# A two-part kernel (chunked scan, then a gated feed-forward layer): decays of first tokens scanned before they are spread, one load of C on ScalarE, three landing times in the planner

## The chip, the cores and the metric

The kernel runs on one core of a Trainium2 chip. The metric is the device time of one execution in microseconds (us), the median of three runs. The core has five engines with their own instruction queues, each strictly in order: PE (TensorE, matmuls; its weight loads are shown apart as PEld), DVE (VectorE), ACT (ScalarE), POOL (GpSimd) and SP (SyncE, which here issues loads and stores). Transfers run on 16 DMA engines.

## The reference

Inputs are x (4, 8, 768, 32), a (4, 8, 768), B and C (4, 8, 768, 16) and three weight matrices (256x1536, 256x1536, 1536x256). A gated linear recurrence runs over each of 32 heads in chunks, and its output, as 3072 tokens of 256 values, goes through a gated feed-forward layer.

```python
log_a = np.log(np.clip(a, 1e-06, 1.0))
for c in range(nc):                               # chunks of a sequence
    cum = np.cumsum(la, axis=-1)
    L = np.exp(cum[:, :, :, None] - cum[:, :, None, :]) * causal
    M = np.einsum('bhin,bhjn->bhij', Cc, Bc) * L
    y_inter = np.einsum('bhin,bhnd->bhid', Cc, state) * np.exp(cum)[..., None]
    y[:, :, sl] = np.einsum('bhij,bhjd->bhid', M, xc) + y_inter
    Bx = (Bc outer xc) * exp(cum[-1] - cum)
    state = exp(sum(la)) * state + sum(Bx)
g = x @ w_gate
out = (g * sigmoid(g) * (x @ w_val)) @ w_out
```

## The kernel before, in words

**Blocks.** The 768 tokens of a sequence are cut into six blocks (k = 0 to 5) of 128 tokens, each of two pieces (q = 0, 1) of 64. A block holds all 4 batches and 8 heads, so it has 512 tokens for the feed-forward layer.

**The scan of a block.** `L` holds the decays between the tokens of a piece, one column row per target token: a row of clipped `a` values is put on all 128 partitions and a `tensor_tensor_scan` with the identity `dj` turns it into products from each source token on (`scan_j`, four scans of 128x520). `E` holds the decays from a piece's first token: the same row for every partition of a head, scanned with `dn` (`scan_n`, one scan of 128x520). B is weighed with the last column of `L` (`weigh_b`), C with `E` (`weigh_c`). `heads_apart` writes C twice, with one or the other head of a pair blanked (`Cz`). PE then makes the scores S, DVE mixes them with `L` (`mix`, four a block), PE makes values and sums of the pieces (the first group of y matmuls), ACT or DVE takes the states T apart, DVE steps them, PE adds what is carried in (the second group of y matmuls).

**How the decays arrive.** For block 0 eight rows of 520 values (`rows`) are loaded twice, clipped, and put on the partitions by a matmul with a 0/1 table `pick` (`spread`, 2 x 4 halves of 260 columns); a ninth such matmul spreads the row that `E` of block 0 is scanned from. For the later blocks everything is loaded once (`all`, 128 partitions x 2 x 195 values), clipped on POOL, written to DRAM (`clipped`), and from there broadcast into `L` (`load_aj`, two transfers) and `E` (`load_an`).

**The feed-forward layer.** f32 weights come as 64-bit words and are taken apart on ACT and DVE into a rounded high part and a low part (per weight piece wg0 to wg11, wo0 to wo5: `w_magnitude`, `w_rest` on ACT, `w_range` on POOL or DVE, `w_shift`, `w_sign`, `w_round` on DVE; the last is the CUSTOM_DVE or ISA row). gate_val makes the gate and the value of weight piece f: in block 0, for the first nine pieces, as two f32 products with the whole x (`xf`) of 4 matmuls, which the profile shows as 8 passes; later as 12 passes of high and low parts (`xh`, `xl`). `silu` is on ACT and `product` on DVE, both into `sg`; they free the two PSUM banks of the piece. There are four such banks, so gate_val of piece f needs silu and product of piece f - 2. `project` makes the output (`po`).

**What sets the order.** Nothing is in program order: every step is an entry `add(engine, cost, run, rank, needs, takes, ...)` of a planner (`Plan`, lines 45 to 180), which keeps a clock for each engine and always issues the step that can start first, by rank among those that can start together. A cost, a rank, a need or a landing time (`lag`) that changes moves steps on all engines. `plan.follow([...])` chains named steps in a fixed order (the lists at lines 949 to 958 and `ORDER`). SP issues the weight loads wg0 to wg11 and the loads of block 1 in the order of `ORDER`. `IDLE` are matmuls on constants ("rest") without a use for the result; lines 963 to 985 hold these tables.

Of the kernel before, what the change touches and what calls it, by code (L numbers as in the profile page):

```python
# [9 lines left out]
F32 = mybir.dt.float32  # L10
# [34 lines left out]
class Plan:  # L45
# [156 lines left out]
def scan_moe_kernel(ctx: ExitStack, tc, aj, an, bc, xb, wgv, wo, cst, own, out):  # L202
# [21 lines left out]
    pick = const.tile([64, BATCH + 1, P], F32, name="pick")  # L224
# [52 lines left out]
    def write_all(e, rows):  # L277
        t = bl[0]["all"][rows].rearrange("p i a t -> p i (a t)")
        e.dma_start(clipped[:, rows].rearrange("i p c -> p i c"), t)
# [12 lines left out]
    def clip(t):  # L292
        ve.tensor_scalar(t, t, 1e-6, 1.0, ALU.max, ALU.min)
# [5 lines left out]
    def scan(t, d):  # L299

        ve.tensor_tensor_scan(t, t, d, 0.0, ALU.mult, ALU.add)

    def clip_rows(i):
        t = bl[0]["rows"]
        t = t[32 * i : 32 * i + H, 0] if i < 2 else t[:H, 1]
        t = t.rearrange("p (g t) -> p g t", t=W)
        clip(t[:, :, 1:] if i < 2 else t[:, 1::K, 1:])
# [3 lines left out]
    def first(b, i):  # L311
        return b < BATCH and not i

    def spread(b, i):

        where, tag = (ps_mm, "mm") if first(b, i) else (ps_at, "at")
        t = bl[0]["spread", b, i] = where.tile([P, HALF], F32, tag=tag, name=f"a{b}_{i}")
        half = slice(HALF * i, HALF * i + HALF)
        if b < BATCH:
            rows = slice(32 * (b % 2), 32 * (b % 2) + H)  # L320
            te.matmul(t, pick[rows, b], bl[0]["rows"][rows, 0, half], start=True, stop=True)
        else:
            r = bl[0]["rows"][:H, 1].rearrange("p (b q t) -> p b q t", b=BATCH, q=K)[:, :, 1]
            te.matmul(t, pick[:H, b], r, start=True, stop=True)

    def scan_spread(b, i):
        if b < BATCH:
            to, d = bl[0]["L"][:, H * b : H * b + H].rearrange("p g t -> p (g t)"), dj
        else:
            to, d = bl[0]["E"].rearrange("p b q t -> p (b q t)"), dn  # L330
        half = slice(HALF * i, HALF * i + HALF)
        d = d.rearrange("p g t -> p (g t)")[:, half]
        ve.tensor_tensor_scan(to[:, half], bl[0]["spread", b, i], d, 0.0, ALU.mult, ALU.add)

# [399 lines left out]
    def do(f, *a):  # L734
        return lambda *e: f(*a, *e)
# [72 lines left out]
    add("SP", 0.48, do(write_all, sp, slice(0, FEW)), -9, ["clipped"], gives="few", lag=2.6)  # L808
    add("Act", 0.1, do(write_all, se, slice(FEW, P)), -1.6, ["clipped", ("rest", 0)], gives="written", lag=0.3)


    for k in range(NB):
# [18 lines left out]
        if not k:  # L831
            add("-", 0.0, lambda: None, -9, takes=[("xl", "rows")], gives="rows", lag=0.2)
            for i in range(3):
                add("DVE", 0.35, do(clip_rows, i), (-9, -8.9, -5)[i], ["rows", *([("scan0", 1)] if i == 2 else [])], gives=("clip", i))
            for b in range(BATCH + 1):
                r = z + 0.5 + b if b < BATCH else -1.3
                for i in range(2 if b < BATCH else 1):
# [74 lines left out]
    for k in range(NB):  # L912
# [39 lines left out]
        ("spread", BATCH, 0), *(("idle", 1, i) for i in range(len(IDLE[1]))), *(("st", 0, b) for b in range(BATCH)),  # L952
# [5 lines left out]
    plan.follow([("L", 0, b) if i else ("scan0", b) for b, i in halves] + [("bt", 0), ("M", 0, 0), ("M", 0, 1), ("E", 0), ("M", 0, 2), ("ce", 0), ("M", 0, 3), ("shift", 0), ("sign", 0, "gate"), ("round", 0, "gate"), ("sign", 0), ("round", 0), ("range", 1)])  # L958
# [4 lines left out]
CST = 2 + 2 * D  # L963
NA = NB * K * BATCH * H // P
IDLE = [-9.0] * 6, [-4.0] * 2
IDLE_AFTER = [], [("spread", BATCH, 0)]
# [12 lines left out]
    [("raw", 8), ("bc", 1), ("raw", 9), ("aj", 1), ("raw", 10), ("xb", 1), ("raw", 11), ("an", 1)],  # L979
# [61 lines left out]
```

## Time and profile before

| | |
|---|---|
| three runs | 351.43, 351.07, 348.14 us, median 351.07 |
| the profiled execution | 349.64 us, span from first to last instruction 347.6 us |
| PE busy | 339.9 us (98%) |
| DVE, ACT, POOL busy | 229.5, 123.7, 44.7 us (66%, 36%, 13%) |
| granted TensorE clock, mean | 1.000 |
| chain that ended last | PE 84%, DMA 5%, DVE 3%, ACT 3% |

The chain of waits is read from the end backwards: whatever released an instruction stands in front of it. From 53.33 us on it consists of PE alone up to the last copy of the output. Timelines give start, duration and, in brackets, the idle time of the engine before the instruction with what ended it. Neighbouring instructions of one kind are merged into one row with their count. A matmul's end is modelled, so the distance between starts is the better measure of PE.

### The profile page before, as it was taken

To read this page: it belongs to the slowest core of one execution; us is meant where nothing else is said; L and a number is where in the kernel's file an instruction comes from. 1 tells how busy PE (TensorE), PEld (TensorE's weight loads), DVE (VectorE), ACT (ScalarE), POOL (GpSimd) and SP (SyncE) were. 2 spreads that over 40 slices of the span, in tenths; PEclk is the share of its full clock that TensorE was granted. 3 is DMA by queue.
4 is the path that set the end of the run, shared out by engine and by line. 5 is a ranking of instruction groups with operands and counts; after the bars stand their busy time and mean duration, and the time that the engine had idled before them with its cause. 6 is when DMAs were issued, how large, how long until landed. Compare 5 with 4: busy or idle time off the path is not lost.

```text
span 347.6 us, 7425 instructions
## 1 busy us (share of the span) xinstructions
PE 339.9 (98%) x3196; PEld 266.3 (77%) x3196; DVE 229.5 (66%) x417; ACT 123.7 (36%) x227; POOL 44.7 (13%) x36
## 2 busy tenths in 40 slices
PE   7999989999999999999999999999999999999996
PEld 6644447888878888878888888888878888888895
DVE  6997999788999792686573676465676430565320
ACT  3795946654336602222322212232212221222221
POOL 2397735322022000000000000000000000000000
PEclk9999999999999999999999999999999999999999
DMA  7999855992001841000561000381000000100001
GB/s 259 294 364 258 231 114 123 272 258 79 0 2 44 190 136 61 0 2 3 152 156 60 0 2 2 100 208 60 1 3 2 2 2 0 60 2 0 0 2 60
DMA packets 9935, 30.98 MB, mean 89 GB/s; under 512 B 1287, under 2 KB 2055, under 8 KB 9263
## 3 DMA queue, kind: packets, MB, share of 16 engines
q1 hardware_dynamic: 7168, 24.23, 23.3%
q0 software_dynamic: 1440, 2.88, 4.9%
q10 hardware_dynamic: 1295, 3.40, 3.2%
q8 instruction: 25, 0.41, 0.5%
q14 instruction: 7, 0.06, 0.1%
HBM read 24.28 MB, written 3.35 MB: 79 GB/s over the span
## 4 chain that ended last, share of the span: by engine, by line
PE 84%; DMA 5%; DVE 3%; ACT 3%; issue 1%; ACTq 0%; DVEq 0%
PE gv L191 50%; PE po L191 29%; PE y L191 4%; DMA wg9r<-in_wgv 4%; PE S L191 1%; DMA wo1r<-in_wo 1%; DVE L L191 1%; DVE wg1w L191 1%; DVE wg0w L191 1%; DVE wg9w L191 0%; DVE sg L191 0%; ACT sg L191 0%; ACT wg9w L191 0%; DVE wg8w L191 0%; DVE E L191 0%
## 5 line engine op out<-in xcount | busy, mean ns | idle before, releaser
L191 DVE TENSOR_TENSOR sg<-gv,sg 128x512 f32<-128x512 f32 x72 | 49.6, 689 | 75.5 <-PE gv L191 73.2
L191 ACT ACTIVATE sg<-gv 128x512 f32<-128x512 f32 x72 | 42.9, 596 | 104.7 <-PE gv L191 104.7
L191 DVE TENSOR_TENSOR hh<-sg,hh 128x512 fp32r<-128x512 f32 x72 | 49.6, 691 | 14.1 <-ACT hh L191 12.8
L191 ACT CAST hh<-sg 128x512 fp32r<-128x512 f32 x32 | 19.9, 622 | 27.1 <-PE po L191 17.5
L191 DVE TENSOR_TENSOR_SCAN L<-L,dj 128x520 f32<-128x520 f32 x20 | 23.9, 1229 | 1.9 <-DMA L<-clipped 1.9
L191 ACT COPY ob<-po 128x512 f32<-128x512 f32 (+1 forms) x13 | 7.2, 555 | 48.7 <-PE po L191 48.2
L191 DVE CAST hh<-sg 128x512 fp32r<-128x512 f32 x40 | 17.4, 435 | 2.4 <-PE po L191 1.2
L191 DVE TENSOR_TENSOR L<-S,L 128x512 f32<-128x512 f32 x24 | 15.2, 684 | 0.3 <-PE S L191 0.3
L191 PE MATMUL po<-hh,wo3h 128*128 128x512 f32 (+1 forms) x52 | 15.2, 375 | 0.0
L191 PE MATMUL po<-hh,wo1h 128*128 128x512 f32 (+1 forms) x52 | 15.2, 375 | 0.0
L191 PE MATMUL po<-hh,wo0h 128*128 128x512 f32 (+1 forms) x52 | 15.2, 375 | 0.0
L191 PE MATMUL po<-hh,wo4h 128*128 128x512 f32 (+1 forms) x52 | 15.1, 373 | 0.0
L191 PE MATMUL po<-hh,wo5h 128*128 128x512 f32 (+1 forms) x52 | 15.1, 373 | 0.0
L191 PE MATMUL po<-hh,wo2h 128*128 128x512 f32 (+1 forms) x52 | 15.0, 373 | 0.0
L191 PE MATMUL y<-L,xb 64*32 64x64 f32 x768 | 11.2, 231 | 0.9 <-DVE L L191 0.9
L191 PEld LDWEIGHTS y<-L,xb 64*32 64x32 f32 x768 | 9.0, 109 | 3.8 <-issue 3.2
L191 PEld LDWEIGHTS po<-hh,wo0h 128*128 128x128 f32 x52 | 9.5, 188 | 1.9 <-issue 0.2
L191 PEld LDWEIGHTS po<-hh,wo4h 128*128 128x128 f32 x52 | 9.5, 188 | 1.7
L191 PEld LDWEIGHTS po<-hh,wo2h 128*128 128x128 f32 x52 | 9.5, 188 | 1.7
L191 PEld LDWEIGHTS po<-hh,wo5h 128*128 128x128 f32 x52 | 9.5, 188 | 1.7
L191 PEld LDWEIGHTS po<-hh,wo3h 128*128 128x128 f32 x52 | 9.4, 188 | 1.8
L191 PEld LDWEIGHTS po<-hh,wo1h 128*128 128x128 f32 x52 | 9.4, 188 | 1.8
(298 smaller groups left out, 750.5 us busy)
## 6 DMA issues: line engine op xcount, KB each, us to landing
L<-clipped SPq DMA_DIRECT2D x10, 520.0 KB, 14.3
xb<-in_xb SPq DMA_DIRECT2D x6, 768.0 KB, 11.2
bc<-in_bc SPq DMA_DIRECT2D x6, 512.0 KB
out<-ob SPq DMA_DIRECT2D x11, 256.0 KB, 2.0
E<-clipped SPq DMA_DIRECT2D x5, 260.0 KB
wg0r<-in_wgv SPq DMA_DIRECT2D x1, 512.0 KB
wg1r<-in_wgv SPq DMA_DIRECT2D x1, 512.0 KB
wg2r<-in_wgv SPq DMA_DIRECT2D x1, 512.0 KB
```

The costliest lines, as they stand in the source:

```text
L191: ins = getattr(self.engine, name)(*a, **k)
```

## The change

The decays from a piece's first token are now scanned once and before they are spread. For blocks 1 to 5 DVE scans the 195 values of each of the 128 partitions of `all[:, 1]` in one instruction (`scan_all`), and ACT writes the result to `clipped[1]`; `load_an` then brings finished decays, so `scan_n` is gone. It waits for that second write ("written e"). For block 0 a new input `first_e` holds 32 rows (batch and head) of 65 values and a 0/1 table; the rows are clipped and scanned as 32x65 (`first_row`), spread by four matmuls of 65 columns into one bank (`spread_e`), and copied to `E` by ACT (`copy_e`). Of the two wide idle matmuls one is left.

`heads_apart` of block 1 may go to ACT alone. `weigh_b` is one instruction for all four batches of a block. The landing times of wg9, of block 1's `L` and of wg10 are given to the planner as 6.1, 2.4 and 1.9 instead of 1.3, 4.8 and 1.3, and a few chains of order are changed. The feed-forward layer is as it was.

```diff
     def load_rows():
...
-        sp.dma_start(t[:H, 1], an[0])
+        sp.dma_start(t[E_ROWS, :W], first_e[:, BATCH * P :])
+        se.dma_start(pick[E_ROWS], first_e[:, : BATCH * P].rearrange("m (b p) -> m b p", p=P))
...
+    def first_row():
+        t = bl[0]["rows"][E_ROWS, :W]
+        clip(t[:, 1:])
+        scan(t, dn[E_ROWS, 0])
+
+    def scan_all():
+        scan(bl[0]["all"][:, 1].rearrange("p a t -> p (a t)"), dn[:, :NA].rearrange("p a t -> p (a t)"))
...
+    def spread_e():
+        t = bl[0]["e"] = ps_at.tile([P, BATCH * W], F32, tag="at", name="e0")
+        for b in range(BATCH):
+            te.matmul(
+                t[:, W * b : W * b + W], pick[E_ROWS, b], bl[0]["rows"][E_ROWS, :W],
+                start=True, stop=True,
+            )
+
+    def copy_e():
+        se.copy(second(bl[0]["E"]).rearrange("p b t -> p (b t)"), bl[0]["e"])
...
-    def scan_n(k):
-
-        scan(bl[k]["E"].rearrange("p b q t -> p (b q t)"), dn.rearrange("p g t -> p (g t)"))
...
-            add("SP", 0.48, do(w_fetch, i), r - 9.0, takes=[("raw", ("raw", i))], gives=("raw", i), lag=1.3)
+            add("SP", 0.48, do(w_fetch, i), r - 9.0, takes=[("raw", ("raw", i))], gives=("raw", i), lag=SHARED.get(i, 1.3))
...
-    add("Act", 0.1, do(write_all, se, slice(FEW, P)), -1.6, ["clipped", ("rest", 0)], gives="written", lag=0.3)
+    add("Act", 0.1, do(write_all, se, 0, slice(FEW, P)), -1.6, ["clipped", ("rest", 0)], gives="written", lag=0.3)
+    add("DVE", 0.48, scan_all, due(0, 1), ["clipped"], gives="products")
+    add("Act", 0.1, do(write_all, se, 1, slice(0, P)), due(0, 1) - 2, ["products"], gives="written e", lag=0.3)
...
+            add("PE", 0.5, spread_e, -1.3, ["row"], takes=[("at", "e")], uses=["e", "rows"], gives="e", kind="s")
+            add("Act", 0.35, copy_e, -1.7, ["e", ("decays", 0)], uses=["e"], gives=("E", 0))
...
-            add("DVE", 1.17, do(scan_n, k), z + 6, [("an", k)], gives=("E", k), slack=SLOW.get(k, 1.0))
...
+        add("DVE", 0.61, do(weigh_b, k), z + 4.5 if k else -1.2, [*(("L", k, b) for b in range(BATCH)), ("xb", k)], gives=("bt", k), slack=SLOW.get(k, 0.0))
+        add([("Act", 1.2)] if k == 1 else [("Act", 1.35), ("DVE", 0.72)], None, do(heads_apart, k), z, [("bc", k)], takes=[("Cz", CZ)], gives=("Cz", k))
...
+E_ROWS = slice(64, 64 + BATCH * H)
-IDLE = [-9.0] * 6, [-4.0] * 2
+IDLE = [-9.0] * 6, [-4.0]
...
+    [("step", 0, 1), "products", ("sign", 2)],
+    [("mag", 6), "written e", ("rest", 7)],
+    [("raw", 8), ("bc", 1), ("raw", 9), ("aj", 1), ("raw", 10), ("xb", 1), ("raw", 11), ("E", 1)],
...
-    [("round", 6), ("Cz", 1)],
+    [("si", 0, 2), ("Cz", 1)],
...
+SHARED = {9: 6.1, "aj": 2.4, 10: 1.9}
```

Three places show what this moves. First DVE in block 0, from the weighing of B to the first weight piece (xb is B and x, bc is B and C, S the scores, a the spread rows), before:

```order
L191 TENSOR_TENSOR xb_100<-xb_100,L_96 128x4x128
L191 TENSOR_TENSOR L_96<-S_0_182,L_96 128x4x2x64
L191 TENSOR_TENSOR L_96<-S_1_183,L_96 128x4x2x64
L191 SCALAR_TENSOR_TENSOR E_97<-a_0_225,dn 128x260
L191 TENSOR_TENSOR L_96<-S_2_184,L_96 128x4x2x64
L191 TENSOR_TENSOR bc_98<-bc_98,E_97 128x4x64
L191 TENSOR_TENSOR L_96<-S_3_185,L_96 128x4x2x64
L191 TENSOR_SCALAR wg0w<-wg0w 128x512
```

and now:

```order
L191 TENSOR_TENSOR xb_101<-xb_101,L_97 128x4x128
L191 TENSOR_TENSOR L_97<-S_0_182,L_97 128x4x2x64
L191 TENSOR_TENSOR L_97<-S_1_183,L_97 128x4x2x64
L191 TENSOR_TENSOR bc_99<-bc_99,E_98 128x4x64
L191 TENSOR_TENSOR L_97<-S_2_184,L_97 128x4x2x64
L191 TENSOR_TENSOR L_97<-S_3_185,L_97 128x4x2x64
L191 TENSOR_SCALAR wg0w<-wg0w 128x512
```

The scan into E left this queue, and the weighing of C moved ahead of the third mix; it now waits for ACT's copy of E. On PE, the one spread matmul and the two wide idle matmuls between the scores and the sums became four narrow spread matmuls and one idle matmul.

Second, ACT from the silu of piece 2 to that of piece 4 and on (xh is the high part of x, wgNh and wgNl high and low parts of weights), before:

```order
L191 ACTIVATE sg_2_466<-gv_2_0_444 128x512
L191 CAST xh_387<-xf 128x512
L191 ACTIVATE wg9w<-wg9r 128x512
L191 ACTIVATE wg9r<-wg9r 128x512
L191 CAST xh_387<-xf 128x512
L191 CAST wg0h<-wg0w 128x512
L191 ACTIVATE sg_3_488<-gv_3_0_473 128x512
```

and now:

```order
L191 ACTIVATE sg_2_469<-gv_2_0_445 128x512
L191 ACTIVATE Cz_473<-bc_437,cs 128x4x128 x2
L191 ACTIVATE wg8r<-wg8r 128x512
L191 CAST xh_389<-xf 128x512 x2
L191 ACTIVATE sg_3_491<-gv_3_0_477 128x512
L191 CAST wg0h<-wg0w 128x512
L191 ACTIVATE wg0l<-wg0w 128x512
L191 CAST wg1h<-wg1w 128x512
L191 ACTIVATE wg1l<-wg1w 128x512
L191 CAST wg2h<-wg2w 128x512
L191 ACTIVATE sg_4_516<-gv_4_0_499 128x512
L191 ACTIVATE wg9w<-wg9r 128x512
```

The two steps on wg9, which wait for its load, stood ahead of the silu of piece 3 and stand behind that of piece 4 now; block 1's Cz, which waits for the load of bc, came in ahead of the silu of piece 3.

Third, DVE in block 0 from the product of piece 4 on, where block 1's decays are scanned, before:

```order
L191 TENSOR_TENSOR sg_4_516<-gv_4_1_513,sg_4_516 128x512
L191 TENSOR_TENSOR xb_452<-xb_452,L_376 128x128 x2
L191 SCALAR_TENSOR_TENSOR L_376<-L_376,dj 128x520
L191 ISA wg7w<-wg7r,wg7w 128x1024
L191 TENSOR_TENSOR xb_452<-xb_452,L_376 128x128
L191 TENSOR_TENSOR sg_5_541<-gv_5_1_536,sg_5_541 128x512
L191 SCALAR_TENSOR_TENSOR L_376<-L_376,dj 128x520
L191 SCALAR_TENSOR_TENSOR E_377<-E_377,dn 128x520
L191 TENSOR_TENSOR xb_452<-xb_452,L_376 128x128
L191 SCALAR_TENSOR_TENSOR wg8w<-wg8r,wg8w 128x512
L191 TENSOR_TENSOR bc_429<-bc_429,E_377 128x512
L191 ISA wg8w<-wg8r,wg8w 128x1024
```

and now, from the rounding of piece 8 on:

```order
L191 ISA wg8w<-wg8r,wg8w 128x1024
L191 TENSOR_TENSOR sg_4_516<-gv_4_1_512,sg_4_516 128x512
L191 SCALAR_TENSOR_TENSOR L_379<-L_379,dj 128x520 x3
L191 TENSOR_TENSOR sg_5_541<-gv_5_1_537,sg_5_541 128x512
L191 SCALAR_TENSOR_TENSOR L_379<-L_379,dj 128x520
L191 TENSOR_SCALAR wg9w<-wg9w 128x512
L191 TENSOR_TENSOR xb_460<-xb_460,L_379 128x4x128
L191 SCALAR_TENSOR_TENSOR wg9w<-wg9r,wg9w 128x512
L191 TENSOR_TENSOR L_379<-S_0_549,L_379 128x4x2x64
L191 TENSOR_TENSOR sg_6_607<-gv_6_1_603,sg_6_607 128x512
L191 ISA wg9w<-wg9r,wg9w 128x1024
L191 TENSOR_TENSOR bc_437<-bc_437,E_380 128x512
```

Pieces 7 and 8 are rounded ahead of all scans of block 1 now, the scan of E is gone, and the weighing of C stands between the first and the second mix.

## Rows read from the trace of the kernel before

**Rows 1.** The page's part 1: busy us (share of the span), xinstructions.
```profile
PE 339.9 (98%) x3196; PEld 266.3 (77%) x3196; DVE 229.5 (66%) x417; ACT 123.7 (36%) x227; POOL 44.7 (13%) x36
```

**Rows 2.** Waits of PE: waiting line <- releaser: us in total, times, longest.
```profile
PE y L191 <- DVE L L191: 0.9, 1, 0.9
```

**Rows 3.** Timeline of PE alone: start, us, instruction, count [idle before <-releaser].
```profile
19.08 3.60 PE L191 MATMUL gv<-xf,wg1w 128*128 128x512 f32 x8
22.71 3.67 PE L191 MATMUL gv<-xf,wg2w 128*128 128x512 f32 x8
26.22 3.60 PE L191 MATMUL gv<-xf,wg3w 128*128 128x512 f32 x8
29.66 3.60 PE L191 MATMUL gv<-xf,wg4w 128*128 128x512 f32 x8
33.50 3.70 PE L191 MATMUL gv<-xf,wg5w 128*128 128x512 f32 x8 [0.25 <-ACT sg L191]
...
41.80 3.60 PE L191 MATMUL gv<-xf,wg7w 128*128 128x512 f32 x8
45.66 3.67 PE L191 MATMUL gv<-xf,wg8w 128*128 128x512 f32 x8 [0.26 <-DVE wg8w L191]
49.26 0.60 PE L191 MATMUL y<-L,xb 64*32 64x64 f32 x18
...
52.04 0.50 PE L191 MATMUL gv<-xh,wg9h 128*128 128x512 f32 x1
53.33 0.39 PE L191 MATMUL gv<-xh,wg9h 128*128 128x512 f32 x1 [0.78 <-issue]
```

**Rows 4.** The chain of waits: start, us, what; the same y group in block 2, and 24 passes.
```profile
102.74 1.41 PE y L191 x90
104.16 5.68 PE po L191 x24
```

**Rows 5.** Timeline of all engines in the first 12 us.
```profile
4.81 1.88 DVE L191 TENSOR_TENSOR_SCAN L<-a,dj 128x260 f32<-128x260 f32 x3 [1.14 <-PE a L191]
...
6.60 0.26 DVE L191 TENSOR_SCALAR rows<-rows 8x256 f32<-8x256 f32 x1
...
9.50 0.50 PEld L191 LDWEIGHTS a<-rows,pick 8*128 8x128 f32 x2 [0.33 <-DVE L L191]
...
10.67 1.03 PE L191 MATMUL rest<-unit 128*128 128x512 bf16 x2
...
11.63 1.15 PE L191 MATMUL st<-xb 64*32 64x64 f32 x62
11.66 0.69 DVE L191 TENSOR_TENSOR_SCAN E<-a,dn 128x260 f32<-128x260 f32 x1
```

**Rows 6.** Busy time by stretch: PE, PEld, DVE, ACT, POOL, PEclk, DMA share, GB/s.
```profile
19.00:22.60 3.60, 3.60 (x9) 1.33 (x7) 3.60 (x11) 3.18 (x6) 3.60 (x3) 1.00 1.02 410
```

**Rows 7.** Timeline, DVE: rounding of weight piece 2.
```profile
21.89 0.68 DVE L191 CUSTOM_DVE_ANT_0 wg2w<-wg2r,wg2w 128x1024 uint16<-128x1024 uint16 x1
```

**Rows 8.** Timeline of all engines, 30 to 46 us: ACT and DVE.
```profile
30.67 0.69 ACT L191 ACTIVATE wg9w<-wg9r 128x512 f32<-128x512 f32 x1 [3.96 <-DMA wg9r<-in_wgv]
30.70 0.88 DVE L191 TENSOR_SCALAR Cz<-bc,cs 128x512 f32<-128x512 f32 x2
...
35.35 2.37 DVE L191 TENSOR_TENSOR_SCAN L<-L,dj 128x520 f32<-128x520 f32 x2
...
44.83 0.69 DVE L191 CUSTOM_DVE_ANT_0 wg8w<-wg8r,wg8w 128x1024 uint16<-128x1024 uint16 x1
```

**Rows 9.** The page: instruction fetches (packets, MB, share); a load (count, KB each, us to landing).
```profile
q8 instruction: 25, 0.41, 0.5%
...
L<-clipped SPq DMA_DIRECT2D x10, 520.0 KB, 14.3
```

**Rows 10.** Timeline of PE alone: the scores of block 0 and of block 1.
```profile
7.57 2.01 PE L191 MATMUL S<-Cz,bc 32*64 32x128 f32 x64
...
37.13 1.21 PE L191 MATMUL S<-Cz,bc 32*64 32x128 f32 x64
```

More of the change, by code (lines that the diff above doesn't have):

```diff
@@ L223, in scan_moe_kernel @@
     step_of = const.tile([P, W], F32, name="step")
-    pick = const.tile([64, BATCH + 1, P], F32, name="pick")
+    pick = const.tile([P, BATCH, P], F32, name="pick")
     dj = const.tile([P, H, W], F32, name="dj")
@@ L275, in load_all, with write_all @@
             sp.dma_start(t[:, i], rows)
-    def write_all(e, rows):
-        t = bl[0]["all"][rows].rearrange("p i a t -> p i (a t)")
-        e.dma_start(clipped[:, rows].rearrange("i p c -> p i c"), t)
+    def write_all(e, i, rows):
+        e.dma_start(clipped[i, rows], bl[0]["all"][rows, i].rearrange("p a t -> p (a t)"))
     def load_bc(k):
@@ L303, in clip_rows @@
     def clip_rows(i):
[L304 to L307, printed above, removed]
+        clip(bl[0]["rows"][32 * i : 32 * i + H].rearrange("p (g t) -> p g t", t=W)[:, :, 1:])
+    def first_row():
[4 more added lines that the diff above has]
+        scan(bl[0]["all"][:, 1].rearrange("p a t -> p (a t)"), dn[:, :NA].rearrange("p a t -> p (a t)"))
@@ L309, in scan_moe_kernel, with first @@
     HALF = H // 2 * W
-    def first(b, i):
-        return b < BATCH and not i
+    def first(i):
+        return not i
     def spread(b, i):
-        where, tag = (ps_mm, "mm") if first(b, i) else (ps_at, "at")
+        where, tag = (ps_mm, "mm") if first(i) else (ps_at, "at")
         t = bl[0]["spread", b, i] = where.tile([P, HALF], F32, tag=tag, name=f"a{b}_{i}")
         half = slice(HALF * i, HALF * i + HALF)
[L319 to L324, printed above, removed]
+        rows = slice(32 * (b % 2), 32 * (b % 2) + H)
+        te.matmul(t, pick[rows, b], bl[0]["rows"][rows, half], start=True, stop=True)
@@ L326, in scan_spread @@
     def scan_spread(b, i):
[L327 to L330, printed above, removed]
+        to = bl[0]["L"][:, H * b : H * b + H].rearrange("p g t -> p (g t)")
         half = slice(HALF * i, HALF * i + HALF)
-        d = d.rearrange("p g t -> p (g t)")[:, half]
+        d = dj.rearrange("p g t -> p (g t)")[:, half]
         ve.tensor_tensor_scan(to[:, half], bl[0]["spread", b, i], d, 0.0, ALU.mult, ALU.add)
+    def spread_e():
[5 more added lines that the diff above has]
+            )
@@ L832, in scan_moe_kernel @@
             add("-", 0.0, lambda: None, -9, takes=[("xl", "rows")], gives="rows", lag=0.2)
[L833 to L837, printed above, removed]
+            for i in range(2):
+                add("DVE", 0.35, do(clip_rows, i), (-9, -8.9)[i], ["rows"], gives=("clip", i))
@@ L838, in scan_moe_kernel @@
+            add("DVE", 0.4, first_row, -8.8, ["rows"], gives="row")
+            for b in range(BATCH):
+                r = z + 0.5 + b
+                for i in range(2):
                     t = ("spread", b, i)
-                    add("PE", 0.25 if first(b, i) else 0.45, do(spread, b, i), r + 0.5 * i, [("clip", b % 2 if b < BATCH else 2), "pick"], takes=[("mm" if first(b, i) else "at", t)], uses=[t, "rows"], gives=t, kind="s")
+                    add("PE", 0.25 if first(i) else 0.45, do(spread, b, i), r + 0.5 * i, [("clip", b % 2), "pick"], takes=[("mm" if first(i) else "at", t)], uses=[t, "rows"], gives=t, kind="s")
@@ L840, in scan_moe_kernel @@
                     need = [t, ("decays", 0)] + ([("scan0", b)] if i else [])
-                    done = ("E", 0) if b == BATCH else ("L", 0, b) if i else ("scan0", b)
-                    add("DVE", 0.63, do(scan_spread, b, i), r + 0.5 * i, need, uses=[t], gives=done)
-        else:
-            add("SP", 0.96, do(load_aj, k), FETCH["aj"] if k == 1 else z - 12, ["few", "written", ("decays", k), *late], gives=("aj", k), lag=4.8)
-            add("SP", 0.48, do(load_an, k), FETCH["an"] if k == 1 else z - 9, ["few", "written", ("decays", k), *late], gives=("an", k), lag=1.8)
+                    add("DVE", 0.63, do(scan_spread, b, i), r + 0.5 * i, need, uses=[t], gives=("L", 0, b) if i else ("scan0", b))
@@ L888, in scan_moe_kernel @@
             mixed = [("M", k, p) for p in range(NP)]
-            weighed = [("bt", k, b) for b in range(BATCH)]
             add("Page", PAGE, lambda: None, z + 3.5, [("S", k, BATCH - 1)], gives=("page", k, 0))
-            add("PE", 1.5, do(values_and_sums, k), z + 11, [("page", k, 0), *mixed, *weighed], takes=[("at", i) for i in y], uses=[L, XB, *y], gives=("st", k, BATCH - 1), kind="f", slack=SLACK)
+            add("PE", 1.5, do(values_and_sums, k), z + 11, [("page", k, 0), *mixed, ("bt", k)], takes=[("at", i) for i in y], uses=[L, XB, *y], gives=("st", k, BATCH - 1), kind="f", slack=SLACK)
             add("Page", PAGE, lambda: None, z + 11, [("st", k, BATCH - 1)], gives=("page", k, 1))
@@ L895, in scan_moe_kernel @@
         if not k:
-            add("-", 0.0, new_whole, -9, [("clip", 2)], takes=[("xl", "xf")], gives="xf")
+            add("-", 0.0, new_whole, -9, [("clip", 1)], takes=[("xl", "xf")], gives="xf")
             add("-", 0.0, do(new_x, 0), due(0, WHOLE) - 9, [("xf", i) for i in range(6)], takes=[("xh", ("xh", 0)), ("xl", ("xl", 0))], gives=("x", 0))
@@ L951, in scan_moe_kernel @@
         *(("spread", b, 1) for b in range(BATCH)), *(("S", 0, b) for b in range(BATCH)),
-        ("spread", BATCH, 0), *(("idle", 1, i) for i in range(len(IDLE[1]))), *(("st", 0, b) for b in range(BATCH)),
+        "e", *(("idle", 1, i) for i in range(len(IDLE[1]))), *(("st", 0, b) for b in range(BATCH)),
         ("vals", 0), ("y", 0, 0), ("vals", 1), ("y", 0, 1),
@@ L957, in scan_moe_kernel @@
         plan.follow(steps)
-    plan.follow([("L", 0, b) if i else ("scan0", b) for b, i in halves] + [("bt", 0), ("M", 0, 0), ("M", 0, 1), ("E", 0), ("M", 0, 2), ("ce", 0), ("M", 0, 3), ("shift", 0), ("sign", 0, "gate"), ("round", 0, "gate"), ("sign", 0), ("round", 0), ("range", 1)])
+    plan.follow([("clip", 0), ("clip", 1), "row"] + [("L", 0, b) if i else ("scan0", b) for b, i in halves] + [("bt", 0), ("M", 0, 0), ("M", 0, 1), ("ce", 0), ("M", 0, 2), ("M", 0, 3), ("shift", 0), ("sign", 0, "gate"), ("round", 0, "gate"), ("sign", 0), ("round", 0), ("range", 1)])
     plan.STAY = {"Act": 0.0, "PE": 0.3}
@@ L963 @@
 CST = 2 + 2 * D
+E_ROWS = slice(64, 64 + BATCH * H)
 NA = NB * K * BATCH * H // P
-IDLE = [-9.0] * 6, [-4.0] * 2
-IDLE_AFTER = [], [("spread", BATCH, 0)]
+IDLE = [-9.0] * 6, [-4.0]
+IDLE_AFTER = [], ["e"]
 FIRST_X = 0, 1, 2, 3, 4, 5
```

33 lines of the change are left out of this document (14 added, 19 removed).

## The prediction

> **What bounds the kernel now.** I read four views, in this order. The busy shares say that PE is busy 98% of the span [rows 1], so only what stands in front of PE counts. The waits of PE name little; the largest behind the first 5 us is 0.9 us for DVE at a y group [rows 2]. That list hides most of the loss, because a modelled matmul end covers short stops. So the third view is the timeline of PE alone, read by the distance between starts. A weight piece of block 0 takes 8 passes, and undisturbed it takes 29.66 - 26.22 = 3.44 us [rows 3]. Against this:
>
> - piece 1 to piece 2: 22.71 - 19.08 = 3.63, 0.19 lost;
> - piece 4 to piece 5: 33.50 - 29.66 = 3.84, 0.40 lost, ended by ACT's silu;
> - piece 7 to piece 8: 45.66 - 41.80 = 3.86, 0.42 lost, ended by DVE's wg8w;
> - the first y group of block 1: 52.04 - 49.26 = 2.78 [rows 3], while the same group of block 2 takes 1.41 [rows 4]: 1.37 lost to DVE's mixes;
> - piece 9: its second pass starts 1.29 after the first [rows 3], where such a pass takes 5.68/24 = 0.24 [rows 4]: 1.05 lost to "issue", a wait for nothing that the profile shows.
>
> Together 3.43 us from 19.08 on. After 53.33 the waits name none, so whatever is won before that point should reach the end whole, and nothing can be won behind it. The fourth view, by stretch, says who is full: from 19.0 to 22.6 DVE is busy 3.60 of 3.60 us, and POOL too [rows 6].
>
> **The change part by part.**
>
> *The start, to the first weight piece: 0.* DVE loses a clip, which held the scans up by 6.79 - 6.60 = 0.19, and the scan into E, 0.60 from start to start (row 0.69) [rows 5]. It gains the clip and scan of 32x65. No row has these shapes; the nearest are the clip of 0.26 and the scan of 260 columns, 1.88/3 = 0.63 [rows 5], so they cost between nothing and 0.9. They stand in DVE's 1.14 us idle ahead of 4.81 [rows 5], and I count them as hidden there; if their load came late they would push all eight scans, up to 0.9.
> PE gives this back. It had one spread matmul of two passes, whose two weight loads took 0.50 [rows 5]; now it has four matmuls, eight weight loads. By that row a load costs 0.22 to 0.25, and 65 columns hide behind it: eight are 1.8 to 2.0. From 9.50 - 0.19 = 9.31 that ends at 11.1 to 11.3. Then one idle matmul: two stood between 10.67 and the sums at 11.63 [rows 5], so 0.45 to 0.48. The sums start at about 11.65, as before (11.63). Bounds: at 10.95 if the narrow matmuls hide, gaining 0.65 (the idle one then waits for the weighing of B, at 10.67 - 0.19); at 12.4 if load and matmul don't overlap, losing 0.8. I take 0, by the weight-load row.
> [...]
> E now reaches DVE through ACT: from 11.2, a copy of about 0.4, so 11.7 instead of 11.47, where DVE would be ready. Of DVE's 0.79 some 0.4 stays.
>
> *Scan of all rows: +0.47 on DVE, 0 to 0.1 on PE.* 195 columns at 0.63 per 260 [rows 5] are 0.47, where DVE is full [rows 6] and PE waits for the rounding that ends at 22.57 [rows 7]. New end: 22.57 - 0.4 + 0.47 = 22.64, so piece 2 starts at about 22.78, 0.07 later.
>
> *ACT: 0.40 won at piece 5.* ACT stood 3.96 us before wg9w, until wg9's load had landed at 30.67 [rows 8], with the silu of piece 3 queued behind it, whose bank piece 5 takes. The step is behind the silu of piece 4 now. What is late next is bc of block 1, for Cz, ahead of the same silu. It is issued before wg9, so it lands before 30.65, and ACT comes to it at about 25.7; between these I take 27. Two Cz at about 0.67, one step of wg8 and two casts follow, and the silu ends near 30.7, 2 us ahead of piece 5 (33.1). Were bc as late as wg9, it would end at 34.1 and cost 1.0.
>
> *DVE: 0.42 at piece 8, 1.37 at y.* Piece 8 is rounded before the scans of block 1, at about 34 instead of 45.5 [rows 8]. DVE also loses Cz (0.88), one scan of the form of L's, 2.37/2 = 1.18 [rows 8], and about 0.3 of the four small weighings. Walked step by step from the rows: L's load, issued at 18.8 and 14.3 in landing [rows 9], is there by 34.5; three scans to 38.4, product 5 to 39.0, the last scan to 40.2, wg9's shift, weighing, sign and first mix to 42.4, product 6, rounding 9 and C to 44.2, two mixes, product 7 and the last mix to 46.6. PE comes to y at 22.78 + 25.5 = 48.3 (six intervals of 3.43 to 3.53 for pieces 2 to 8, 3.5 for the last, 1.14 for the scores). So 1.7 us are to spare.
>
> *"Issue": 0.75 of 1.05.* Fetches of instructions are in the trace: 25 packets of 16 KB [rows 9] for 2 x 3196 matmul and load instructions [rows 1], one for 256. A y group is 256 of them in 1.41 us, so two fetches come close together there, and the stop behind it fits that. [...] I keep 0.3.
> [...]
>
> *Later blocks: 0.* DVE loses 1.18 per block, off PE's path. In block 2 the weighing of C now stands ahead of the scans of L and waits for E's load there; what it holds up, product 5 of block 1, is needed only when piece 7 takes its bank.
>
> Sum: -0.07 + 0.40 + 0.42 + 1.37 + 0.75, and 0.2 because three groups no longer start from a stop (22.71 to 26.22 is 3.51, against 3.44) = 3.1 us. The profiled execution would go from 349.64 to 346.5. It lies 1.43 below the median of the runs; the four times known (351.43, 351.07, 348.14, 349.64) have a mean of 350.07, and I take the sum from there: **347.0**, 1.2% below the median of 351.07.
>
> **The rivals.**
>
> [...]
> - *Instruction fetches set the distance.* From the y group to the second pass of piece 9 took 53.33 - 49.26 = 4.07. If that is the least between two fetches, removing DVE's stop only lengthens the other. Then 1.0 is won, up to y: 349.1. For it: the stop stands behind 256 fast instructions; against: block 2 shows none.
> [...]
> - *The gains aren't there*, since ACT waits for bc or DVE is late again: 0.5 won, 349.6.
> - *Slower: E of block 1 comes late.* Its load now waits on SP for the write of the scanned array, which ACT issues at about 22.9 into full queues. If write and load each take the 14.3 of L [rows 9], E lands at 51.5; C stands ahead of three mixes on DVE, and PE stops at y for about 6.3 us: 353.3. It costs one for one from 45.2 on and decides the sign from 48.3. Against: the broadcast of E is half of one of L's two, and the write has 100 KB.
>
> **How the numbers follow.** Chances: forecast 0.45, start 0.12, fetches 0.20, clock 0.10, no gains 0.08, slower 0.05. The three runs differ by 3.3 us, which each case carries. Range 344.2 to 350.3: the lower end is 346.3 less 2, the upper takes in the fetches, the clock and the missing gains with about 0.7 to 1. About 1% (3.5 us) is what a measurement of this kernel can tell from no change. Faster by more means below 347.5: three quarters of the forecast (0.34), nearly all of the start case (0.11), a little of the others (0.04): 0.49. Slower by more: 0.05. Within: 0.46.
>
> **What would show it.** Sums of block 0 at 11.5 to 11.8; piece 2 at 22.5 to 22.9; no ACT wait for wg9, one of 1 to 2 us for bc; pieces 5 and 8 at 3.4 to 3.55 after the ones ahead; the first y group of block 1 in 1.4, starting near 48.3; the second pass of piece 9 near 50.2 instead of 53.33; from there on the same distances as before. Wrong would be: a new stop of PE at y or piece 9, or a first weight piece later than 16.

## The result, and the profile after

The changed kernel takes 353.44 us in the median of 22 runs (350.19 to 356.1), the kernel before 351.4 (22 runs, 348.08 to 354.47): ratio 1.0059, 95% interval 1.0032 to 1.0086. It is 0.6% slower; 347.0 was forecast. (A ratio leaves disturbed runs out, so it is not always the quotient of the medians.) The profiled execution took 350.19 us, span 348.1, against 349.64 and 347.6.

Part 1 of the profile page after answers to [rows 1]: five PE instructions more, 4.1 us less of DVE.

```profile
PE 340.8 (98%) x3201; PEld 267.2 (77%) x3201; DVE 225.4 (65%) x399; ACT 123.7 (36%) x227; POOL 44.7 (13%) x36
```

PE's timeline after, 15 to 60 us, answers to [rows 3]:

```profile
15.80 3.70 PE L191 MATMUL gv<-xf,wg0w 128*128 128x512 f32 x8
19.34 3.60 PE L191 MATMUL gv<-xf,wg1w 128*128 128x512 f32 x8
22.84 3.67 PE L191 MATMUL gv<-xf,wg2w 128*128 128x512 f32 x8
26.35 3.60 PE L191 MATMUL gv<-xf,wg3w 128*128 128x512 f32 x8
29.79 3.60 PE L191 MATMUL gv<-xf,wg4w 128*128 128x512 f32 x8
33.22 3.60 PE L191 MATMUL gv<-xf,wg5w 128*128 128x512 f32 x8
...
41.42 3.60 PE L191 MATMUL gv<-xf,wg7w 128*128 128x512 f32 x8
44.85 3.60 PE L191 MATMUL gv<-xf,wg8w 128*128 128x512 f32 x8
48.38 0.90 PE L191 MATMUL y<-L,xb 64*32 64x64 f32 x60
...
49.89 0.73 PE L191 MATMUL gv<-xh,wg9h 128*128 128x512 f32 x2
50.46 0.62 PE L191 MATMUL gv<-xl,wg9h 128*128 128x512 f32 x2
...
53.37 0.74 PE L191 MATMUL gv<-xh,wg10h 128*128 128x512 f32 x2 [0.47 <-ACT wg10h L191]
55.04 0.73 PE L191 MATMUL gv<-xh,wg10l 128*128 128x512 f32 x2 [0.46 <-DVE wg10l L191]
...
58.72 0.73 PE L191 MATMUL gv<-xh,wg11h 128*128 128x512 f32 x2
```

Four later rows of the kernel before, in the same view, to compare with:

```profile
53.55 0.63 PE L191 MATMUL gv<-xl,wg9h 128*128 128x512 f32 x2
...
60.28 0.73 PE L191 MATMUL gv<-xh,wg11h 128*128 128x512 f32 x2
...
95.87 1.21 PE L191 MATMUL S<-Cz,bc 32*64 32x128 f32 x64
...
102.67 0.80 PE L191 MATMUL y<-L,xb 64*32 64x64 f32 x60
```

Pieces 5 and 8 come 3.43 us after the ones ahead and the y group takes 1.51: the gains are there. The third pass of piece 9 (`gv<-xl,wg9h`) starts at 50.46, before at 53.55: 3.09 us ahead, the forecast 3.1. Two new stops at piece 10 leave 60.28 - 58.72 = 1.56, still there at the scores of block 2 (94.30 against 95.87). Then PE's timeline of block 2 after answers to [rows 4] (`hh` are the parts of the gated product that the output product takes):

```profile
94.30 1.21 PE L191 MATMUL S<-Cz,bc 32*64 32x128 f32 x64
99.08 0.50 PE L191 MATMUL po<-hh,wo0h 128*128 128x512 f32 x1 [0.62 <-ACT hh L191]
100.17 0.51 PE L191 MATMUL po<-hh,wo0h 128*128 128x512 f32 x1 [0.59 <-DVE hh L191]
101.97 0.50 PE L191 MATMUL po<-hh,wo1h 128*128 128x512 f32 x1 [0.16 <-DVE hh L191]
103.32 0.80 PE L191 MATMUL y<-L,xb 64*32 64x64 f32 x60
```

From scores to y are 9.02 us, before 6.80: 2.2 lost, and the lead of 1.57 has become a lag of 0.65. The profiled executions differ by 0.55. DVE's timeline after shows where it comes from (wo2 to wo4 are weight pieces of the second product):

```profile
76.30 0.43 DVE L191 CAST hh<-sg 128x512 fp32r<-128x512 f32 x1
79.20 0.69 DVE L191 TENSOR_TENSOR bc<-bc,E 128x512 f32<-128x512 f32 x1 [2.48 <-DMA E<-clipped]
79.81 0.69 DVE L191 TENSOR_TENSOR wo2l<-wo2w,wo2h 128x512 fp32r<-128x512 f32 x1
...
83.24 0.43 DVE L191 TENSOR_SCALAR wo3w<-wo3w 128x512 int32<-128x512 int32 x1 [0.82 <-POOL wo3w L191]
...
95.97 0.43 DVE L191 TENSOR_SCALAR wo4w<-wo4w 128x512 int32<-128x512 int32 x1 [2.14 <-POOL wo4w L191]
96.31 0.68 DVE L191 TENSOR_TENSOR sg<-gv,sg 128x512 f32<-128x512 f32 x1
96.91 0.68 DVE L191 SCALAR_TENSOR_TENSOR wo4w<-wo4r,wo4w 128x512 int32<-128x512 int32 x1
97.62 0.69 DVE L191 CUSTOM_DVE_ANT_0 wo4w<-wo4r,wo4w 128x1024 uint16<-128x1024 uint16 x1
98.23 1.28 DVE L191 TENSOR_TENSOR L<-S,L 128x512 f32<-128x512 f32 x2
```

and DVE's timeline before:

```profile
97.06 2.48 DVE L191 TENSOR_TENSOR L<-S,L 128x512 f32<-128x512 f32 x4 [0.32 <-PE S L191]
...
100.06 0.42 DVE L191 TENSOR_SCALAR wo4w<-wo4w 128x512 int32<-128x512 int32 x1
```

The weighing of C waits 2.48 us for E of block 2, with wo2l, wo3 and wo4 behind it. In the new order the shift of wo4 stands ahead of product 11 (`sg<-gv,sg`), and its two other steps ahead of the mixes (`L<-S,L`). So DVE waits 2.14 us for POOL's wo4w, and the mixes start at 98.23, 3.9 us after the scores' start; before, they stood ahead of wo4 and began at 97.06, 1.2 us after the scores' start. The `hh` that PE stops for are made between the mixes and behind them.

The profiled run is the best of the 22. It accounts for 0.55 of the 2.0 us between the medians, and there is no trace of a longer run of this kernel. Two more things, seen in the traces of other kernels below, may stand behind the rest; that they do is not shown.

### The profile page after: what moved, and what is told of

It is laid out like the page before. It is cut to its first block, busy times and chain, and to the rows that moved or that the text cites. A ratio compares the mean times of both kernels' runs of the same rounds, so it can differ in the third digit from the quotient of the medians.

```text
span 348.1 us, 7424 instructions
## 1 busy us (share of the span) xinstructions
PE 340.8 (98%) x3201; PEld 267.2 (77%) x3201; DVE 225.4 (65%) x399; ACT 123.7 (36%) x227; POOL 44.7 (13%) x36
## 3 DMA queue, kind: packets, MB, share of 16 engines
HBM read 24.33 MB, written 3.35 MB: 80 GB/s over the span
## 4 chain that ended last, share of the span: by engine, by line
PE 82%; DVE 9%; DMA 3%; ACT 3%; issue 2%; POOL 1%; DVEq 0%; ACTq 0%
PE gv L191 47%; PE po L191 27%; PE y L191 5%; DVE L L191 3%; DMA wg11r<-in_wgv 3%; PE S L191 2%; DVE sg L191 1%; PE a L191 1%; DMA rows<-in_aj 1%; POOL wo4w L191 1%; PE e L191 1%; DVE hh L191 1%; DVE wg11w L191 0%; DVE wo4w L191 0%; DVE wo3w L191 0%
```

## The experiments

Each kernel ran 12 times beside the kernel before, whose medians were 350.64 (e1 to e4), 350.75 (e5 to e8), 350.92 (e9 to e12) and 351.95 (e13 to e15). Three distances from each profile stand beside the times: the start of weight piece 1; from the y group of block 1 to the third pass of piece 9; from the scores of block 2 to its y. The last column counts runs whose mean granted clock lay under 0.9965 (every run has 0.995 or less, or 0.998 or more); for the kernel before it takes all four sets of runs.

| kernel | median us | ratio (95%) | piece 1 at | y1 to piece 9 | S2 to y2 | under 0.9965 |
|---|---|---|---|---|---|---|
| before | 351.4 | 1 | 19.08 | 4.29 | 6.80 | 30 of 134 |
| after | 353.44 | 1.0059 (1.0032-1.0086) | 19.34 | 2.08 | 9.02 | 10 of 22 |
| e1 | 351.05 | 0.9997 (0.9961-1.0033) | 22.64 | 2.08 | 7.23 | 2 of 12 |
| e2 | 351.03 | 1.0023 (0.9983-1.0063) | 23.25 | 4.35 | 6.80 | 4 |
| e3 | 352.07 | 0.9995 (0.9951-1.004) | 19.60 | 4.71 | 7.22 | 3 |
| e4 | 353.18 | 1.008 (1.0046-1.0113) | 19.73 | 3.49 | 10.83 | 9 |
| e5 | 350.93 | 0.9995 (0.9962-1.0029) | 21.69 | 4.58 | 6.81 | 6 |
| e6 | 350.13 | 0.9959 (0.9925-0.9994) | 21.10 | 3.91 | 7.18 | 1 |
| e7 | 348.94 | 0.9936 (0.9904-0.9967) | 19.36 | 3.22 | 6.80 | 0 |
| e8 | 349.24 | 0.9949 (0.9922-0.9977) | 19.34 | 3.55 | 6.80 | 0 |
| e9 | 348.98 | 0.9974 (0.9936-1.0013) | 19.25 | 2.08 | 6.80 | 0 |
| e10 | 347.97 | 0.9941 (0.9907-0.9974) | 21.71 | 2.08 | 6.80 | 0 |
| e11 | 350.0 | 1.0003 (0.997-1.0037) | 19.58 | 3.35 | 6.81 | 0 |
| e12 | 352.6 | 1.0069 (1.0031-1.0106) | 22.27 | 2.08 | 9.11 | 0 |
| e13 | 348.67 | 0.9943 (0.9908-0.9979) | 19.70 | 2.08 | 6.80 | 0 |
| e14 | 349.33 | 0.994 (0.9909-0.9971) | 20.28 | 2.08 | 6.80 | 0 |
| e15 | 350.69 | 0.9987 (0.9956-1.0018) | 21.74 | 2.07 | 6.81 | 0 |

**Block 2: e1 and e2.** One chained order is added to the changed kernel in each.

```diff
+    plan.follow([("L", 2, 3), ("ce", 2)])        # e1
+    plan.follow([("M", 2, 3), ("shift", 16)])    # e2
```

> The weighing of C of block 2 is moved behind block 2's four scans of L on DVE. Three theories of why the changed kernel is 2.1 us slower. Theory A (the load): DVE's 2.48 us wait for E of block 2 delays everything behind it (wo2l, wo3, wo4) and so the mixes of block 2. Theory B (the order): what costs is that the steps of wo4, which wait 2.14 us for POOL, now stand ahead of the mixes of block 2. Theory C (the start): the narrow spreads and the one idle matmul less cost about 2 us in most runs, whatever block 2 does. Here A expects the stops of PE in the po group ahead of y of block 2 (1.4 us in three stops) to go, and 1.4 to 2.2 us less (ratio to the kernel before about 1.000). B expects DVE to wait for POOL's wo4w again, at least 1 us of the stops to stay, and less than 0.7 us won (ratio 1.004 to 1.006). C expects no change (1.006).

> The four mixes of block 2 are put ahead of the steps of wo4 on DVE; the weighing of C still waits for E of block 2. Theory B (the order) expects the stops of PE in the po group ahead of y of block 2 to go and 1.4 to 2.2 us less (ratio to the kernel before 1.000 to 1.002). Theory A (the load) expects wo4, late by the 2.48 us wait and now 2.5 us later still, to stop PE where wo4 is first used, with under 0.7 us won (1.004 to 1.006). Theory C (the start) expects no change (1.006).

In both traces the stops of PE are gone. In e1 DVE's waits for E of block 2 and for POOL's wo4w are both gone, as theory A had it and B not. In e2 the wait for E is even longer, yet PE stops nowhere in block 2, as B had it and A not. DVE's waits in e2 (us in total, times, longest):

```profile
DVE bc L191 <- DMA E<-clipped: 3.2, 1, 3.2
```

So each theory seems to be half of it: the late load makes wo4 late, and the new order lets wo4's lateness reach the mixes. Both medians are 2.4 us below the changed kernel's. By the ratios e1 won 2.2 us and e2 only 1.3, and both intervals overlap the changed kernel's. In both traces PE also came later to the scores of block 2 than in after's (96.79 and 99.75 against 94.30), which by itself can give DVE time (e3 below shows it). e15 tests the order of block 2 without this doubt.

**Piece 10 and the start: e3 and e4.** Of e4's edit only the line on the idle matmuls is shown.

```diff
+    plan.follow([("round", 10), ("shift", 11)])   # e3
-IDLE = [-9.0] * 6, [-4.0]                         # e4, with spread, scan and order
+IDLE = [-9.0] * 6, [-4.0] * 2                     # of E of block 0 as before
```

> On DVE the rounding of wg10 is put ahead of the shift and the weighing of wg11, to take away the two stops of 0.47 and 0.46 us at piece 10 of block 0 (about 1.3 us of PE's distance). If nothing behind absorbs it, 1.0 to 1.3 us are won (ratio 1.002 to 1.003). If the chain on DVE and POOL that ends at the mixes of block 2 sets the time there (theories A and B), PE only comes earlier to a stop that ends at the same moment: 0 to 0.3 us won in this run (1.005 to 1.006), and the stops ahead of y of block 2 grow by about 1 us.

> The start of the kernel before (E of block 0 spread raw and scanned on DVE, two idle matmuls) with all the rest of the change. Theory C (the start) expects 1.5 to 2.1 us less (ratio 1.000 to 1.002) and the first weight piece 0.2 to 0.3 us earlier in the profile. Theories A and B expect at most the 0.25 us by which the first weight piece comes earlier (ratio about 1.005), if the stops in block 2 stay.

In e3 the two stops at piece 10 went, and its ratio (0.9995) lies below both branches. Its profile shows a stop that after's had not: 2.28 us "issue" inside the y group. By stretch (PE, PEld, DVE, ACT, POOL, clock, DMA share, GB/s):

```profile
48.00:50.00 2.00, 2.00 (x127) 1.36 (x126) 1.97 (x5) 1.36 (x3) 1.70 (x1) 1.00 0.05 8
50.00:52.00 2.00, 0.19 (x21) 0.04 (x4) 1.97 (x4) 0.62 (x1) 0.26 (x1) 1.00 0.00 0
52.00:54.00 2.00, 1.53 (x7) 1.20 (x7) 1.97 (x6) 1.28 (x4) 0.00 (x0) 0.79 0.03 8
54.00:56.00 2.00, 2.00 (x6) 1.51 (x6) 2.00 (x9) 1.03 (x3) 1.79 (x2) 0.50 0.23 39
```

PE is busy for 0.19 of 2 us, and behind it the granted clock falls to 0.50: in the timeline the passes of piece 9 then come 0.85 us per pair instead of 0.46. So PE reached the scores of block 2 2.9 us later than in after's trace, DVE waited only 0.23 us for E there, and S2 to y2 was 7.22, though the order of block 2 is the changed kernel's: what block 2 loses depends on when PE comes. In e4 a like fall of the clock came behind the stops of block 2 (PE busy 0.50 from 99 to 101, clock 0.59 and 0.55 behind), so S2 to y2 grew to 10.83. The old start saved nothing here, against theory C; but block 2's longer loss makes e4 a poor measure of the start, and e7 below speaks the other way.

**The three orders together, and the fetch: e5 to e8.** e5 has the orders of e1, e2 and e3; e6 adds the second idle matmul, e7 the old start; e8 adds to e5:

```diff
-        times, wide = (1, 512) if n else (4, 64)
+        times, wide = (1, 512) if n else (1, 128)
```

> Three orders on DVE together: C of block 2 behind block 2's scans, block 2's mixes ahead of wo4, wg10's rounding ahead of wg11's steps. If what block 2 gave back is all that stood between forecast and result, the won 2 to 3 us of block 0 now show: 0.991 to 0.995 of the kernel before, few runs at a mean clock under 0.9965. If the start (clock later) or the fetch stop behind the y group of block 1 takes as much in most runs, 0.997 to 1.000.

> As the three orders together, with the second idle matmul ahead of the sums of block 0 again (0.48 us of PE). If the missing one lets the pace of PE rise later in many runs (3.3 us from the first weight piece to the second in one of the profiles), the median is 1 to 2 us better than with one; if not, 0.2 to 0.5 us worse.

> As the three orders together, with the start of the kernel before (E of block 0 spread raw, scanned on DVE, two idle matmuls), and so with PE's instruction count in front as before. If the new start costs, it is 1 to 2 us better than the three orders with the new start; if the start is neutral, within 0.5 us of it. A stop of 1 us or so is expected at the second or third pass of piece 9, at the same instruction as in the kernel before, in some runs.

> As the three orders together, with 18 of the 24 idle matmuls at the very start left out (6 of 128 columns instead of 24 of 64), so that all PE instructions behind stand 36 earlier against the blocks of 256 in which they are fetched: the block that began at the end of the y group of block 1 now begins in piece 10. If the stop named issue is the fetch of that block, it does not appear (y group to second pass of piece 9 in 1.9 to 2.1 us) and the median is 0.5 to 1.5 us below the three orders alone, with fewer runs of a lower mean clock. If the stop has another cause, 0 to 2.3 us of it stay at the end of the y group and the times are as without the shift.

e5 won little over e1 and e2 (its second branch): piece 1 began 5.38 us after piece 0 and the stop behind y was there, in the same place as in e2 and e3:

```profile
51.56 0.80 PE L191 MATMUL y<-xb 64*32 64x64 f32 x59
54.59 0.30 PE L191 MATMUL y<-xb 64*32 64x64 f32 x3 [2.24 <-issue]
54.82 0.73 PE L191 MATMUL gv<-xh,wg9h 128*128 128x512 f32 x2
```

In e6, with one matmul more in front, the stop stands one matmul earlier (after 58 of these instead of 59), and its median, 0.8 us below e5's, cannot be told from no change. (The 3.3 us of e6's expectation is how much later piece 1 started in e1 than in after, 22.64 against 19.34; piece 0 took 5.40 there.) With the kernel before's count of PE instructions (e4, e7), ten fewer in front, it stands five matmuls later, in piece 9, near the place of [rows 3]. With the shift it is gone: y1 to piece 9 is 2.08 in every trace of e9 to e15 but e11's, and what e8 and e11 have above that lies at a wait for DVE's mixes. All 96 runs of the eight shifted kernels kept a mean clock above 0.9965. e8 is 1.7 us below e5. So the stop is tied to the place in the instruction stream, as a fetch for every 256 instructions would be (an estimate: the page of after counts 25 packets for 2 x 3201 instructions of PE and PEld); that a fetch stands at the stop is not shown.

e7 is 2.0 us below e5 and as fast as e8, without the shift and with no run of a lower clock, as its expectation had it for a start that costs. e13 and e10, both shifted, differ in the start, too, and their ratios are alike. So the new start seems to cost through the place where its ten instructions put the stop, at the end of the y group instead of in piece 9; no run parts the two further. The shift itself shows in the time only between e5 and e8, not between the kernel before and e11 or between the changed kernel and e12.

**What is left, and how far it goes: e9 to e12.** e9 adds to e8

```diff
+    plan.follow([("M", 1, 3), ("ce", 1)])
+    plan.follow([("si", 0, 6), ("mag", 11), ("rest", 11)])
```

e10 has these with the old start and scans `all` behind the rounding of wg2; e11 and e12 are the kernel before and the changed one with the shift alone.

> The three orders with the shifted fetch blocks, and two more orders in block 0: C of block 1 weighed behind the mixes of block 1 (DVE waited 0.86 us for E of block 1 ahead of them in the run with the shift) and the two steps of wg11 on ACT behind the silu of piece 6 (ACT waited 3.8 us for wg11's load ahead of it). If these waits cost what the trace shows (y group of block 1 in 2.99 instead of 1.4 us, piece 7 to piece 8 in 4.09 instead of 3.44), 1.0 to 1.8 us are won against the shift: median 347.4 to 348.2, ratio 0.989 to 0.992. If the loads only come late in some runs, 0 to 0.7 us.

> The same five orders and the shift with the start of the kernel before, and the scan of all rows behind the rounding of wg2, where it held up piece 2 by 0.85 us. Against the three orders with the old start (348.94): 0.8 won at piece 2, 0.5 to 1 at piece 9 by the shift: 347.2 to 348.0. If the new start costs nothing by itself, within 0.4 us of the same with the new start; if it lets the pace rise later in a good part of the runs, 0.5 to 1.5 us better.

> The kernel before with nothing but the shift (6 idle matmuls of 128 columns at the very start instead of 24 of 64). If the stop at piece 9 is the fetch of a block of instructions, it goes: up to 1.05 us less, 0.4 to 1.0 in the median (ratio 0.997 to 0.999). By the rival that the least distance between two fetches sets the time from the y group, nothing is won.

> The changed kernel with nothing but the shift; block 2 keeps its late mixes. If the loss in block 2 (2.2 us in the profile, more where the clock falls behind it) and the fetch stop are separate, the stop behind the y group of block 1 goes, the stops in the po group of block 2 stay, and the median lies 0.7 to 1.7 us below 353.4 (ratio 1.001 to 1.004), with a lower mean clock in a third to half of the runs. If the fetch stop is what costs in most runs, 1.000 or less.

e9 lies 0.3 us below e8 in the median, above it by ratio: nothing was won that can be told. In its trace the two losses that its expectation names are gone (2.08, and 3.43 from piece 7 to piece 8), and a stop of 1.0 us for wg2w stands at piece 2: DVE took longer for the scan of all rows and for the rounding (last row) than in after's trace (0.55 and 0.68).

```profile
20.56 0.97 DVE L191 TENSOR_TENSOR_SCAN all<-all,dn 128x195 f32<-128x195 f32 x1
21.45 0.66 DVE L191 SCALAR_TENSOR_TENSOR wg2w<-wg2r,wg2w 128x512 int32<-128x512 int32 x1
22.03 0.67 DVE L191 TENSOR_SCALAR wg3w<-wg3w 128x512 int32<-128x512 int32 x1
22.61 1.08 DVE L191 CUSTOM_DVE_ANT_0 wg2w<-wg2r,wg2w 128x1024 uint16<-128x1024 uint16 x1
```

e10 is the fastest by its median, 0.6% below the kernel before with an interval under 1; the ratios of e7, e8, e13 and e14 are nearly the same. e11 cannot be told from the kernel before (a stop of 2.7 us for wg8w in its profile hides what it may have won). e12 keeps block 2's loss (9.11) and is still slower than before. Its stop behind the y group is gone and no run has a lower clock, yet its ratio is not below the changed kernel's (1.0069 against 1.0059), where 1.001 to 1.004 was expected. By these runs that stop and the clock behind it do not account for the changed kernel's time.

**The last open points: e13 to e15.** e13 is e10 with the new start, e14 that with two idle matmuls, e15 the changed kernel with e2's order and the shift alone.

> The five orders, the shift and the later scan of all rows, with the new start (E of block 0 scanned before it is spread, one idle matmul). It differs from the best run so far (347.97) in the start alone. If the new start is neutral, as forecast, 347.5 to 348.5; if it costs by itself (narrow spreads, one idle matmul less, a later rise of the pace), 348.7 to 350.

> The same with two idle matmuls ahead of the sums of block 0. If the pace of PE rises late in many runs because one is missing, 0.7 to 1.5 us better than with one; if not, 0 to 0.5 us worse, since the sums start 0.3 to 0.48 us later.

> The changed kernel with only two edits: block 2's mixes ahead of wo4, and the shift. If late mixes of block 2 and the fetch stop are the two things that ate the gain, these two edits alone bring it to 349.2 to 350.2 (ratio 0.995 to 0.998), the two small stops at piece 10 remaining; if the earlier landing of E or wg10's order is needed too, 350.5 or more.

e13 and e10 lie 0.7 us apart with ratios of 0.9943 and 0.9941: no difference can be told. e14 gained nothing in the median. e15 is e12 with the order of block 2 mended and nothing else. PE came to the scores at 96.66 and 97.16; S2 to y2 fell from 9.11 to 6.81 (in e2, with the same order, DVE's wait for E stayed, at 3.2 us), and the ratios, 0.9987 and 1.0069, have intervals that don't overlap. So the order alone costs some 2 to 3 us (1.9 by the medians, 2.9 by the ratios). e13 has the order too, and loses nothing there although PE comes to the scores at 93.49, earlier than in after's trace. e15's median lies in its second branch; that wg10's order makes the difference to e8 is not shown, as their intervals overlap. All of PE's waits in e13:

```profile
PE a L191 <- DVE rows L191: 1.5, 1, 1.5
PE rest L191 <- DVE warm L191: 1.1, 1, 1.1
PE po L191 <- issue: 0.8, 1, 0.8
```

## Why the prediction was wrong

- **The sum up to piece 9 (3.1 us): right in the profiled run.** Pieces 5 and 8 came at 3.43, where 3.4 to 3.55 was forecast; y began at 48.38 (48.3), the third pass of piece 9 at 50.46 (the second was forecast for 50.2).
- **"Later blocks: 0": the step that failed.** It saw that C of block 2 would wait for E, and followed that wait to product 5 alone. Behind it on DVE stood wo2l, with wo3, POOL and wo4 in a chain, and the new order had put wo4 ahead of block 2's mixes: 2.2 us in after's trace, 2.3 between e12 and e15. The order of block 2 could have been read beforehand; I read it in block 0 alone.
- **"From there on the same distances": wrong at piece 10.** PE came 3.1 us earlier to piece 10, but wg10's rounding on DVE, which stands behind the steps of wg11 and product 8, only 1.0 us earlier (51.99 instead of 53.02): 1.5 us lost. I did not ask what is late next behind piece 9.
- **"Issue", 0.75 of 1.05: mis-sized, and no constant.** The 0.3 that I kept of it was an estimate, and no run shows it: the 1.05 was won whole in after and e1, but 1.8 to 2.6 us were lost in e2, e3, e5 and e6. If these stops are fetches, the ten instructions more put one boundary into piece 8 and, 256 further on, one into the last matmuls of the y group, where they stand, still behind fast instructions. The loss that the rival with 0.20 named, a longer stop by PE's fetches, came in four of these six traces; its least distance of 4.07 did not hold, as after and e1 took 2.08 to the third pass. 10 of after's 22 runs had a lower mean clock, none of e12's 12; but e12 is no faster.
- **The start, 0: right by itself as far as is shown.** Sums at 11.82, eight weight loads in 1.78 (0.22 each), as forecast; the 0.65 for narrow matmuls that hide, which the 346.3 of the range takes from 347.0, did not show. e10 and e13, both shifted, do not differ; e5 and e7, unshifted, do, by 2.0 us, which the sum did not foresee.
- **The scan of all rows, -0.07: mis-sized.** Piece 1 to piece 2 took 3.50 in after, but 4.20 in e4, 4.37 in e7 and 4.60 in e9. The rounding of wg2 took 1.08 instead of 0.68 in e7 and e9, the 195-column scan 0.97 instead of 0.55 in e9; in e4 PE stopped 0.60 us for wg2w. With the scan behind the rounding (e10, e13) it is 3.43 and 3.44.
- **The slower rival, E of block 1 late (0.05): not the cause.** DVE did wait 0.86 us for it in e8, in no case 6.3. It named the right load in the wrong block.

What stays open: the 1.5 us between the medians that the profiled run does not have. One candidate is how often the pace of PE rises late at the start. Piece 0 took 5.2 to 5.4 us instead of 3.5 in e1, e2, e5 and e15 (new start) and in e10 (old one), 4.9 in e12, though the mean granted clock of these profiled executions is 1.000 (0.999 in e12); in e6 it took 5.3 by a stop of 1.61 named "issue". The case that the chances call the clock, a first piece at a slower pace (compare [rows 10]), would lie there, with up to 1.9 us. One profile for each kernel can't say whether the new start makes it likelier, and no run settled the share of this in after's median. With nearly all stops mended, e10 and e13 won 0.6% over the kernel before, 2.0 us, not the 3.1 of the sum; where the last 1 us went is open too.

## What to carry to other kernels

Where a change moves a step that waits for a load ahead of other work on an in-order queue, follow everything queued behind it, two or three hand-overs far, and read the new order at every later place that this reaches, above all where a planner decides it. A gain read from one trace counts only if its stop comes at the same size in other runs; an "issue" stop behind hundreds of short instructions did not (0 to 2.6 us here). A wait that is gone in one trace may be gone only because the waiting engine came later (e3): compare kernels in which it comes at the same time (e12, e15). Removing one stop can expose the next deadline a few microseconds on, as at piece 10 here (stops of 0.47 and 0.46 us): list what must be ready there before adding the gain to the sum.

## What the runs showed of the hardware

- A stop named "issue" comes at a fixed place in PE's instruction stream, behind some 256 instructions in 1.4 us, and costs 0 to 2.6 us in kernels with the same instructions there (after, e1, e2, e3, e5). With 18 matmuls and their loads fewer in front (36 instructions) it left that place in all eight kernels; smaller ones came in or behind the y group of block 2 instead (0.3 us in e11, 0.8 to 1.4 us in e8, e9, e13, e14 and e15).
- Behind a stop of 2.28 us (PE busy for 0.19 of 2 us) the granted clock went to 0.50 (e3); behind stops of 1.26 and 0.59 (0.50 of 2 us) to 0.59 and 0.55 (e4). In e5, behind 2.24 us (0.36 of 2 us), the passes of piece 9 came 0.46 us per pair, and the profiled execution has a mean granted clock of 1.000. e3's stop and the slow passes behind it cost 4.1 us up to piece 10, against e1. e12's shorter stops in block 2 (0.69 and 0.59) had no such sequel in 12 runs (mean clock 0.999 or more).
- The scan of 128x195 took 0.55 us in after, e7 and e10, and 0.97 in e9; the rounding of a weight piece (128x1024) took 0.68 (before, after) or 1.08 to 1.10 (e7, e9, e10) at the same place (wg2).
